# Two of eight pairs of output weight rows prepared inside the last expert, the others spread over sixteen chunks, and the last pair of token blocks finished product by product

## The chip, the core and the metric

The program runs on one core of one Trainium2 chip. The metric is the device time of one execution in microseconds (us). The engines are TensorE (PE in the rows; PEld is its weight load), VectorE (DVE), ScalarE (ACT), GpSimd (POOL) and SyncE (SP), which issues the loads.

## The reference, cut to what matters

Three layers run one after the other: a windowed attention, a mixture of eight experts of which each token takes one, and a dense layer with a squared rectifier. The change is in the third layer and in what is prepared for it.

```python
def _moe_ref(x, w_gate, w_output_gate, w1, w2):   # x: 2304 tokens x 512
    ...
    for e in range(E):                            # 8 experts
        mask = e_idx == e
        h = np.maximum(x[mask] @ w1[e], 0.0)      # 512 -> 1024
        ye = h @ w2[e]                            # 1024 -> 512
        out[mask] = gate_w[mask, None] * eom[mask, e, None] * ye

def _moe2_ref(x, w_in, w_out):
    h = x @ w_in                                  # 512 -> 2048
    r = np.maximum(h, 0.0)
    g = r * r
    return (g @ w_out).astype(np.float32)         # 2048 -> 512
```

The scale of a token (`gate_w` times `eom`) is positive, so the kernel leaves it out of the experts and multiplies its square onto the last layer's result (`gs`).

## The kernel before

Every float32 operand of a product is split into two float16 parts, hi and lo, and a product is three matmuls (hi by hi, hi by lo, lo by hi; `SPLIT`). ScalarE writes hi, VectorE then writes lo as operand minus hi.

**The experts.** Tokens are gathered expert by expert. Expert r has two layers on TensorE: eight groups for 1024 hidden rows (line 1172), then four groups for 512 outputs (line 1193), whose results go to `x2`. The experts take 264, 440, 248, 380, 284, 340, 304 and 320 tokens as columns. Beside the matmuls a `Stream` of small steps runs: pieces of the coming experts' weights are loaded by SP into four staging buffers and split (lines 300 and 301), and sixteen pieces of `w_in`, which arrive as 64-bit numbers, are decoded by three VectorE operations (lines 328, 332 and 336) and split (lines 342 and 343) into `wi`. `mixture` deals the `w_in` pieces to the 16 half-experts by a share called `spare`, in which the last expert counts twice; it gets 3 of the 16. The method `to(part, frac)` of the stream issues steps up to a fraction of a part, in program order, between the kernel's own instructions. An engine runs its instructions in that order.

**The dense layer.** The first four blocks of 128 tokens (`G0`) run plainly: for each of 16 chunks of 128 hidden rows, `plain1` makes h by 12 matmuls of 512 columns (line 1257), ScalarE squares it and VectorE splits it (line 1282), and `plain2` adds its product with `w_out` into four accumulators `acc`, 12 matmuls again (line 1289). `plain2` runs three chunks behind `plain1` (`AHEAD`), and takes the hidden rows n and n + 8 of pair n one after the other (`ORDER1`). The other 14 blocks run in seven pairs of blocks, each in 8 steps: `pair1` makes h for the hidden rows n and n + 8, and `pair2` multiplies 2 by 2 blocks with seven products in place of eight, into seven halves of the four banks `acc` (line 1327). For that, `shared_out` prepares `w_out` in eight pairs of hidden rows: two pieces decoded and split into `wo` (lines 342 and 343), four sums of 256 columns (line 376), and the sums split into `wt`. Its steps run in the plain stage, `bg.to(0, (i + 2) / NF)` ahead of the i-th `plain2`.

**The end of a pair of blocks.** After the last step n = 7 the seven products are combined: ScalarE copies p1 (line 1335), VectorE makes six sums (line 816), ScalarE scales two results by `gs` (line 1344), and GpSimd scatters them to the output (line 1248).

Of the kernel before, what the change touches and what calls it, by code (L numbers as in the profile page):

```python
# [114 lines left out]
def fused_kernel(ctx: ExitStack, tc: tile.TileContext, q, k, v, w_gate, w_ogate, w1, w2, w_in, w_out, out):  # L115
# [247 lines left out]
    def shared_out(wo, wt, tmp):  # L363

        res = []
        for n in range(HF):
            x = [None, None]

            def whole(i, n=n, x=x):
                parts(x[i](), wo[:, 0, n + HF * i, :], wo[:, 1, n + HF * i, :], WO_S)  # L370

            def sums(x=x):
# [5 lines left out]
            def sum_parts(n=n):  # L378
                parts(tmp, wt[:, 0, n], wt[:, 1, n], WO_S)

            if wide:
                src = w_out.bitcast(U32).rearrange("(k p) c -> k p c", p=P)
                for i in range(2):
                    st = {}
                    load, ops = decode64(src[n + HF * i], st)
                    x[i] = lambda st=st: st["d"].bitcast(F32)
                    res.append((load, ops + [lambda i=i, whole=whole: whole(i)] + [sums, sum_parts][:2 * i]))
            else:
                st = {}

                def load(n=n, st=st):
                    st["t"] = stage_p.tile([P, 1024], F32, tag="stage", name="stage")
                    for i in range(2):
                        k = n + HF * i
                        nc.sync.dma_start(out=st["t"][:, i * DM:(i + 1) * DM], in_=w_out[k * P:(k + 1) * P, :])
                for i in range(2):
                    x[i] = lambda i=i, st=st: st["t"][:, i * DM:(i + 1) * DM]
                res.append((load, [lambda whole=whole: whole(0), lambda whole=whole: whole(1), sums, sum_parts]))
        return res

# [403 lines left out]
    x2 = [w_p.tile([P, KC, XW], F16, name=f"x2{i}") for i in range(2)]  # L804

# [153 lines left out]
    wu = [g_p.tile([P, 8192], F16, name=f"wu{i}") for i in range(3)]  # L959
    xg = [g_p.tile([P, DM], F32, name=f"xg{i}") for i in range(4)]  # L960
# [156 lines left out]
    def mixture(caps, e_regs, first):  # L1117
# [167 lines left out]
    def plain2(n, g, ps):  # L1285
        f = ORDER1[n]
        for j in range(G0):
            for k, (a, o) in enumerate(SPLIT):
                nc.tensor.matmul(out=ps[j], lhsT=g[:, a, j * P:(j + 1) * P], rhs=wo[:, o, f, :],  # L1289
                                 start=n == 0 and k == 0, stop=n == NF - 1 and k == 2)  # L1290
# [28 lines left out]
    def pair2(u, n, g, ps):  # L1319
        for left, right, b, h in PRODUCTS:  # L1320
            for k, (a, o) in enumerate(SPLIT):
                if isinstance(right, tuple):
                    i, c = right
                    r = wo[:, o, n + HF * i, c * HD:(c + 1) * HD]
                else:
                    r = wt[:, o, n, right]
                nc.tensor.matmul(out=ps[b][:, h * HD:(h + 1) * HD], lhsT=g[:, a, left * P:(left + 1) * P], rhs=r,  # L1327
                                 start=n == 0 and h == 0 and k == 0,
                                 stop=n == HF - 1 and k == 2 and (h == 1 or b == 3))
        if n < HF - 1:  # L1330
            return
        (p1, p2), (p6, p7), (p5, p3), (p4, _) = [(x[:, 0:HD], x[:, HD:]) for x in ps]
        c1, u2, u3, v = [tmp[:, i] for i in range(4)]
        x1, x2_ = out_tile(), out_tile()
# [58 lines left out]
```

## Time and profile before

| what | us |
|---|---|
| median of 3 runs | 783.53 |
| the three runs | 783.53, 783.87, 779.66 |
| the profiled execution | 779.48 |
| its span, first to last instruction | 777.80 |
| in it: last expert, first and second layer | 349.09 to 376.5 |
| in it: the plain stage, 16 chunks | 376.55 to 498.41 |
| in it: seven pairs of blocks | 498.41 to 766.88 |
| in it: the last results' way out | 766.88 to 777.80 |
| TensorE busy over the span | 724.6 (93%) |
| VectorE busy over the span | 479.0 (62%) |
| ScalarE busy over the span | 398.8 (51%) |

The span leaves 1.68 us of the execution's own time outside. The granted TensorE clock is given as a share of full speed; its two levels are 1.2 and 2.4 GHz, and its mean over the span was 0.962. A busy TensorE is not TensorE at its peak: a matmul that waits inside, or runs at the lower clock, counts as busy.

### The profile page before, as it was taken

Reading aid. Unit: us, or ns where it says so; the run is one execution under the profiler, and the core shown is the slowest. Engines: PE = TensorE matmul, PEld = TensorE weight load, DVE = VectorE, ACT = ScalarE, POOL = GpSimd, SP = SyncE. Lnnn points to the kernel's source line nnn. Section 1 sums busy time; section 2 is a strip of 40 time slices with the busy share of each in tenths; the row PEclk is TensorE's granted clock in tenths of the full one; section 3 lists DMA queues with packets and bytes.
Section 4 is the critical chain, followed back from the end, with each engine's and each line's share of the span. In section 5 each row is a group of like instructions: output and inputs, shape, how many; then the busy total and the mean of one; then the engine's idle time right before and its main releaser. Section 6 shows DMA issues by size and latency. Waiting matters only on the chain.

```text
span 777.8 us, 16191 instructions
## 1 busy us (share of the span) xinstructions
PE 724.6 (93%) x6460; PEld 550.5 (71%) x6460; DVE 479.0 (62%) x1081; ACT 398.8 (51%) x762; POOL 68.9 (9%) x125
## 2 busy tenths in 40 slices
PE   7998997699999989999888887999999999999994
PEld 5877886385596677777433334788888888888883
DVE  4677678488689798765366667544444444454542
ACT  5786776265475465453434444544444444445351
POOL 8000002320110020000000000100000000000000
PEclk7999998599999999999989999899999999999998
DMA  9996543777676675652222220000000000000000
GB/s 218 203 220 152 128 105 86 236 241 264 198 252 212 200 238 183 212 162 73 85 81 82 81 82 0 29 28 14 15 14 15 8 22 1 29 1 29 1 28 28
DMA packets 74979, 82.74 MB, mean 106 GB/s; under 512 B 33784, under 2 KB 57848, under 8 KB 74896
## 3 DMA queue, kind: packets, MB, share of 16 engines
q1 hardware_dynamic: 71552, 71.61, 31.5%
q0 software_dynamic: 3344, 10.01, 3.7%
q8 instruction: 53, 0.87, 0.5%
q14 instruction: 30, 0.25, 0.1%
HBM read 72.16 MB, written 9.44 MB: 105 GB/s over the span
## 4 chain that ended last, share of the span: by engine, by line
PE 69%; DVE 11%; DMA 8%; ACT 8%; issue 3%; SPq 0%; POOL 0%; POOLq 0%; DVEq 0%; ACTq 0%
PE l L1257 18%; PE acc L1327 14%; PE bank L1193 13%; PE bank L1172 11%; DMA vt<-in_v_dram 3%; PE sps L584 2%; PE xps L629 2%; DMA q<-in_q_dram 2%; PE acc L1289 2%; PE tps L610 2%; ACT w L1266 1%; ACT w L1265 1%; DVE dec L336 1%; DVE dec L332 1%; PE bank L978 1%
## 5 line engine op out<-in xcount | busy, mean ns | idle before, releaser
L1257 PE MATMUL l<-x,wi 128*128 128x256 f16 (+1 forms) x1536 | 200.0, 286 | 1.2 <-DVE x L1199 1.2
L1257 PEld LDWEIGHTS <-wi 128*128 128x128 f16 x1536 | 150.5, 98 | 41.0 <-issue 3.1
L1327 PEld LDWEIGHTS <-gg 128*128 128x128 f16 x1176 | 114.9, 98 | 17.3 <-issue 3.1
L1193 PE MATMUL bank<-hs,wu 128*128 128x264 f16 (+7 forms) x768 | 109.3, 300 | 2.4 <-DVE hs L1176 2.2
L1172 PE MATMUL bank<-xs,wu 128*128 128x264 f16 (+7 forms) x768 | 108.6, 303 | 1.2 <-ACT wu L300 0.8
L816 DVE TENSOR_TENSOR w<-w 128x128 f32<-128x128 f32 x224 | 55.3, 288 | 81.4 <-ACT w L1266 79.0
L1172 PEld LDWEIGHTS <-wu 128*128 128x128 f16 x768 | 75.7, 99 | 32.3 <-ACT wu L300 1.1
L1311 DVE TENSOR_TENSOR gg<-w,gg 128x896 f16<-128x896 f32 x56 | 61.2, 1092 | 60.5 <-ACT gg L1310 60.5
L1193 PEld LDWEIGHTS <-wu 128*128 128x128 f16 x768 | 74.8, 98 | 31.9 <-issue 2.5
L1327 PE MATMUL acc<-wt,gg 128*128 128x256 f16 x672 | 92.6, 272 | 1.1 <-DVE A L816 0.5
L1310 ACT ACTIVATE gg<-w 128x896 f16<-128x896 f32 x56 | 53.2, 950 | 64.6 <-DVE w L816 64.6
L301 DVE SCALAR_TENSOR_TENSOR wu<-stage,wu 128x1024 f16<-128x1024 f32 (+1 forms) x68 | 75.8, 1127 | 12.5 <-ACT wu L300 11.9
L1265 ACT ACTIVATE w<-l 128x512 f32<-128x512 f32 x72 | 42.5, 591 | 64.5 <-PE l L1257 59.8
L1327 PE MATMUL acc<-wo,gg 128*128 128x256 f16 x504 | 73.3, 272 | 0.0
L1289 PE MATMUL acc<-wo,gg 128*128 128x512 f16 x192 | 52.0, 420 | 18.6 <-ACT wo L342 16.1
L300 ACT ACTIVATE wu<-stage 128x1024 f16<-128x1024 f32 (+1 forms) x68 | 65.3, 974 | 4.2 <-DMA stage<-in_moe_w_dram 4.2
L1289 PEld LDWEIGHTS <-gg 128*128 128x128 f16 x192 | 20.1, 105 | 47.7 <-issue 30.6
L1175 ACT ACTIVATE hs<-bank 128x264 f16<-128x264 f32 (+7 forms) x64 | 27.8, 436 | 39.6 <-PE bank L1172 39.6
L1266 ACT ACTIVATE w<-w 128x512 f32<-128x512 f32 x72 | 45.4, 630 | 2.3
L601 ACT ACTIVATE pr<-sps,mx 128x96 f32<-128x96 f32 x144 | 37.1, 349 | 13.0 <-DVE mx L592 9.6
L970 POOL DMA_INDIRECT xg<-x_dram,slot_i x24 | 27.0, 1127 | 152.8 <-PE bank L978 99.0
L1198 ACT ACTIVATE x<-bank 128x264 f32 (+7 forms) x32 | 14.1, 440 | 51.4 <-PE bank L1193 51.4
(192 smaller groups left out, 796.9 us busy)
## 6 DMA issues: line engine op xcount, KB each, us to landing
stage<-in_moe_w_dram SPq DMA_DIRECT2D x62, 512.0 KB
dstage<-in_moe_w_in_dram SPq DMA_DIRECT2D x16, 512.0 KB
dstage<-in_moe_w_out_dram SPq DMA_DIRECT2D x16, 512.0 KB
vt<-in_v_dram SPq DMA_DIRECT2D x56, 96.0 KB
q<-in_q_dram SPq DMA_DIRECT2D x16, 288.0 KB
k<-in_k_dram SPq DMA_DIRECT2D x16, 288.0 KB
x_dram<-xn SPq DMA_DIRECT2D x22, 128.0 KB
hs<-in_moe_w_dram SPq DMA_DIRECT2D x2, 512.0 KB
```

Source lines behind the costliest of these rows:

```text
L300: nc.scalar.activation(out=half(hi, n), in_=sv, func=AF.Copy, scale=scale)
L301: nc.vector.scalar_tensor_tensor(out=half(lo, n), in0=sv, scalar=scale, in1=half(hi, n), op0=ALU.mult, op1=ALU.subtract)
L816: V.tensor_tensor(out=out, in0=a, in1=b, op=op)
L1172: nc.tensor.matmul(out=ps, lhsT=w[:, a, k, f * P:(f + 1) * P], rhs=x[:, k, 0:C], start=nn == 0, stop=nn == 3 * KC - 1)
L1193: nc.tensor.matmul(out=ps, lhsT=w[:, a, f, c * P:(c + 1) * P], rhs=hs[:, o, f, 0:C], start=nn == 0, stop=nn == 3 * (F // P) - 1)
L1257: nc.tensor.matmul(out=ps, lhsT=wi[:, a, kc, f * P:(f + 1) * P], rhs=x2[o][:, kc, toks], start=nn == 0, stop=nn == 11)
L1265: nc.scalar.activation(out=flat[:, 512:], in_=ps, func=AF.Relu, scale=R_D)
L1266: nc.scalar.activation(out=flat[:, 0:512], in_=flat[:, 512:], func=AF.Square)
L1289: nc.tensor.matmul(out=ps[j], lhsT=g[:, a, j * P:(j + 1) * P], rhs=wo[:, o, f, :], start=n == 0 and k == 0, stop=n == NF - 1 and k == 2)
L1310: nc.scalar.activation(out=g[:, 0], in_=w7, func=AF.Copy)
L1311: V.tensor_tensor(out=g[:, 1], in0=w7, in1=g[:, 0], op=ALU.subtract)
L1327: nc.tensor.matmul(out=ps[b][:, h * HD:(h + 1) * HD], lhsT=g[:, a, left * P:(left + 1) * P], rhs=r, start=n == 0 and h == 0 and k == 0, st ...
```

## The change

The buffer `wu1`, one of three that hold expert weights, moves to a pool that lives on into the dense layer. `shared_out` takes a list of pairs and issues its steps one by one: hi of both pieces, the sums, hi of the sums, and then the lo parts. In the last expert, where no `w_in` piece remains, two pairs are prepared into `wu1`, one in each layer; the sixteen `w_in` pieces go to experts 0 to 6. The other six pairs are prepared in the plain stage into a tile `wp`, an equal share of steps ahead of each of the 16 chunks, beginning with the first. Of the last pair of blocks, the steps n = 6 and 7 are merged: each of the seven products runs over both before the next. At the end of every pair of blocks the scaling by `gs` goes into VectorE's sums, with three small ScalarE operations of 256 columns in place of two of 512, and the sums stand in another order; the fourth sum of `w_out` changes its sign, so that p4 is added.

```diff
-    def shared_out(wo, wt, tmp):
+    def shared_out(ns, wo, wt, tmp):
         res = []
-        for n in range(HF):
+        for n in ns:
...
-            def whole(i, n=n, x=x):
-                parts(x[i](), wo[:, 0, n + HF * i, :], wo[:, 1, n + HF * i, :], WO_S)
+            def hi(i, n=n, x=x):
+                nc.scalar.activation(out=wo(n)[:, 0, i], in_=x[i](), func=AF.Copy, scale=WO_S)
+
+            def lo(i, n=n, x=x):
+                nc.vector.scalar_tensor_tensor(out=wo(n)[:, 1, i], in0=x[i](), scalar=WO_S, in1=wo(n)[:, 0, i],
+                                               op0=ALU.mult, op1=ALU.subtract)
...
-                for out, p, q in ((t[0], b12, b11), (t[1], b22, t[0]), (t[2], b22, b12), (t[3], t[1], b21)):
-                    nc.vector.tensor_tensor(out=out, in0=p, in1=q, op=ALU.subtract)
+                out, p, q = ((t[0], b12, b11), (t[1], b22, t[0]), (t[2], b22, b12), (t[3], b21, t[1]))[m]
+                nc.vector.tensor_tensor(out=out, in0=p, in1=q, op=ALU.subtract)
...
+            ops = ([lambda m=m, sums=sums: sums(m) for m in range(4)]
+                   + [sum_hi, lambda lo=lo: lo(0), lambda lo=lo: lo(1), sum_lo])
...
-                    res.append((load, ops + [lambda i=i, whole=whole: whole(i)] + [sums, sum_parts][:2 * i]))
+                    res.append((load, dec + [lambda i=i, hi=hi: hi(i)] + ops * i))
...
-        spare = [max(caps[h // 2] - 240, 0) * (1 if h < 2 * E - 2 else 2) for h in range(2 * E)]
+        spare = [max(caps[h // 2] - 240, 0) * (h < 2 * E - 2) for h in range(2 * E)]
+        outs = shared_out(range(NE), lambda n: wo_part(wu1, n), lambda n: wt_part(wu1, n),
+                          xg_t[:, 0:2].rearrange("p a (s d) -> p (a s) d", s=2))
...
+            if h >= 2 * E - 2:
+                m = len(outs) // (2 * E - h)
+                part += outs[:m]
+                del outs[:m]
...
-    wo = m2_p.tile([P, 2, NF, DM], F16, name="wo")
-    wt = m2_p.tile([P, 2, HF, 4, HD], F16, name="wt")
-    tmp = m2_p.tile([P, 4, HD], F32, name="tmp")
-    bg = Stream([shared_out(wo, wt, tmp)])
+    wp = m2_p.tile([P, (HF - NE) * WP], F16, name="wp")
+    tmp = m2_p.tile([P, 5, HD], F32, name="tmp")
...
+    bg = Stream([shared_out(range(NE, HF), wo, wt, tmp[:, 0:4])])
...
-    def pair2(u, n, g, ps):
+    def pair2(u, ng, ps):
         for left, right, b, h in PRODUCTS:
-            for k, (a, o) in enumerate(SPLIT):
...
+            for n, g in ng:
+                for k, (a, o) in enumerate(SPLIT):
...
         nc.scalar.activation(out=c1, in_=p1, func=AF.Copy)
-        tt(x1[:, 0:HD], p2, c1, ALU.add)
+        nc.scalar.activation(out=c1g, in_=p1, func=AF.Copy, scale=g1)
         tt(u2, p6, c1, ALU.add)
         tt(u3, p7, u2, ALU.add)
+        nc.scalar.activation(out=u3, in_=u3, func=AF.Copy, scale=g0)
+        scaled(x1[:, 0:HD], p2, g1, c1g)
         tt(v, p5, u2, ALU.add)
-        tt(x2_[:, HD:], p5, u3, ALU.add)
-        tt(x1[:, HD:], p3, v, ALU.add)
-        tt(x2_[:, 0:HD], u3, p4, ALU.subtract)
-        for x, j in ((x1, u + 1), (x2_, u)):
-            nc.scalar.activation(out=x, in_=x, func=AF.Copy, scale=gs[:, j:j + 1])
-            send(x, j)
+        nc.scalar.activation(out=v, in_=v, func=AF.Copy, scale=g1)
+        scaled(x0[:, HD:], p5, g0, u3)
+        scaled(x1[:, HD:], p3, g1, v)
+        send(x1, u + 1)
+        scaled(x0[:, 0:HD], p4, g0, u3)
+        send(x0, u)
...
-        bg.to(0, (i + 2) / NF)
+        bg.to(0, (i + 1) / NF)
...
+        elif i < len(steps) - 2:
+            pair2(u, [(n, g_of.pop(i))], ps)
+        elif n == HF - 1:
+            pair2(u, [(m, g_of.pop(i + m - n)) for m in (n - 1, n)], ps)
```

**VectorE in the plain stage.** `gg` is the lo part of a chunk's squares, `dec` a decoded piece, `wo` and `wt` (before) or `wp` (after) the prepared rows. Before, two chunks and the pair between them:

```order
L1282 TENSOR_TENSOR gg<-w_8207,gg 128x512
L328 TENSOR_SCALAR dec<-dstage 128x512
L332 SCALAR_TENSOR_TENSOR dec<-dstage,dec 128x512
L336 SCALAR_TENSOR_TENSOR dec<-dstage,dec 128x512
L343 SCALAR_TENSOR_TENSOR wo<-dec,wo 128x512
L328 TENSOR_SCALAR dec<-dstage 128x512
L1282 TENSOR_TENSOR gg<-w_8248,gg 128x512
L332 SCALAR_TENSOR_TENSOR dec<-dstage,dec 128x512
L336 SCALAR_TENSOR_TENSOR dec<-dstage,dec 128x512
L343 SCALAR_TENSOR_TENSOR wo<-dec,wo 128x512
```

VectorE in the plain stage after the change, from the second to the third chunk:

```order
L1316 TENSOR_TENSOR gg<-w_8208,gg 128x512
L336 SCALAR_TENSOR_TENSOR dec<-dstage,dec 128x512
L381 TENSOR_TENSOR tmp<-dec 128x256
L381 TENSOR_TENSOR tmp<-dec,tmp 128x256
L381 TENSOR_TENSOR tmp<-dec 128x256
L381 TENSOR_TENSOR tmp<-dec,tmp 128x256
L1316 TENSOR_TENSOR gg<-w_8233,gg 128x512
L374 SCALAR_TENSOR_TENSOR wp<-dec,wp 128x512 x2
L387 SCALAR_TENSOR_TENSOR wp<-tmp,wp 128x1024
L328 TENSOR_SCALAR dec<-dstage 128x512
```

A lo part no longer stands right behind the decode whose hi part it waits for, and the preparation begins three chunks earlier.

**VectorE from expert 3 to expert 4.** `x_2755` is an expert's result, `wu` expert weights, `hs` the hidden rows that the second layer reads. Before:

```order
L1199 SCALAR_TENSOR_TENSOR x_2755<-bank,x_2754 128x380
L343 SCALAR_TENSOR_TENSOR wi<-dec,wi 128x512
L301 SCALAR_TENSOR_TENSOR wu_2886<-stage,wu_2886 128x1024
L1199 ISA
L1199 SCALAR_TENSOR_TENSOR x_2755<-bank,x_2754 128x380
L301 SCALAR_TENSOR_TENSOR wu_2886<-stage,wu_2886 128x1024 x2
L1176 SCALAR_TENSOR_TENSOR hs<-bank,hs 128x284
```

VectorE at the same place, after:

```order
L1227 SCALAR_TENSOR_TENSOR x_2755<-bank,x_2754 128x380
L301 SCALAR_TENSOR_TENSOR wu_2887<-stage,wu_2887 128x1024
L328 TENSOR_SCALAR dec<-dstage 128x512
L332 SCALAR_TENSOR_TENSOR dec<-dstage,dec 128x512
L1227 ISA
L1227 SCALAR_TENSOR_TENSOR x_2755<-bank,x_2754 128x380
L336 SCALAR_TENSOR_TENSOR dec<-dstage,dec 128x512
L343 SCALAR_TENSOR_TENSOR wi<-dec,wi 128x512
L301 SCALAR_TENSOR_TENSOR wu_2887<-stage,wu_2887 128x1024
L1204 SCALAR_TENSOR_TENSOR hs<-bank,hs 128x284
```

A second `w_in` piece has come into expert 3, and the end of it stands ahead of expert 4's first hidden rows.

**VectorE at the end of the last pair of blocks.** `A` and `ob` are the two result tiles. Before:

```order
L816 TENSOR_TENSOR A<-acc_11680,tmp 128x256
L816 TENSOR_TENSOR tmp<-acc_11681,tmp 128x256
L816 TENSOR_TENSOR tmp<-acc_11681,tmp 128x256
L816 TENSOR_TENSOR tmp<-acc_11682,tmp 128x256
L816 TENSOR_TENSOR ob_8070<-acc_11682,tmp 128x256
L816 TENSOR_TENSOR A<-acc_11682,tmp 128x256
L816 TENSOR_TENSOR ob_8070<-tmp,acc_11683 128x256
```

VectorE at the same place, after:

```order
L831 TENSOR_TENSOR tmp<-acc_11727,tmp 128x256
L831 TENSOR_TENSOR tmp<-acc_11727,tmp 128x256
L1374 SCALAR_TENSOR_TENSOR A<-acc_11726,gs,tmp 128x256
L831 TENSOR_TENSOR tmp<-acc_11728,tmp 128x256
L1374 SCALAR_TENSOR_TENSOR ob_8154<-acc_11728,gs,tmp 128x256
L1374 SCALAR_TENSOR_TENSOR A<-acc_11728,gs,tmp 128x256
L1374 SCALAR_TENSOR_TENSOR ob_8154<-acc_11729,gs,tmp 128x256
```

The operation that reads the first bank (the first row before) now stands third, and no operation of 512 columns follows on ScalarE.

## Rows read from the trace of the kernel before

**Rows 1.** The page, part 4: the chain that ended last, by engine

```profile
PE 69%; DVE 11%; DMA 8%; ACT 8%; issue 3%; SPq 0%; POOL 0%; POOLq 0%; DVEq 0%; ACTq 0%
```

**Rows 2.** Busy time by stretch; columns in the first row

```profile
core 0: us, PE busy (x) PEld busy (x) DVE busy (x) ACT busy (x) POOL busy (x), PEclk, DMA share, GB/s
...
277.90:293.14 15.24, 13.08 (x111) 10.56 (x110) 14.53 (x26) 9.69 (x17) 4.45 (x3) 1.00 0.80 263
...
362.13:376.55 14.42, 13.20 (x98) 9.33 (x96) 7.78 (x14) 3.96 (x8) 0.00 (x0) 1.00 0.08 18
376.55:498.41 121.86, 103.31 (x481) 48.70 (x482) 75.97 (x135) 54.02 (x83) 0.00 (x0) 0.93 0.19 64
498.41:757.70 259.29, 258.22 (x2343) 228.91 (x2342) 123.05 (x303) 122.98 (x177) 15.95 (x16) 1.00 0.05 17
```

**Rows 3.** Timeline of TensorE, plain stage: start, us, instruction, idle time before and its releaser

```profile
392.25 5.58 PE L1289 MATMUL acc<-wo,gg 128*128 128x512 f16 x12 [5.18 <-ACT wo L342]
...
405.97 0.38 PE L1289 MATMUL acc<-wo,gg 128*128 128x512 f16 x1
...
431.74 0.38 PE L1289 MATMUL acc<-wo,gg 128*128 128x512 f16 x1 [1.76 <-ACT wo L342]
```

**Rows 4.** The chain that ended last, plain stage and end: start, us, what

```profile
400.78 2.59 PE acc L1289 x12
403.37 2.60 PE l L1257 x12
...
768.67 0.27 issue
```

**Rows 5.** Groups by line, 376.55 to 498.41: busy us, mean ns, then idle before

```profile
L1289 PE MATMUL acc<-wo,gg 128*128 128x512 f16 x192 | 52.0, 420 | 18.6 <-ACT wo L342 16.1 <-DVE wo L343 2.1
...
L1282 DVE TENSOR_TENSOR gg<-w,gg 128x512 f16<-128x512 f32 x16 | 11.1, 692 | 21.4 <-ACT gg L1281 21.4
L336 DVE SCALAR_TENSOR_TENSOR dec<-dstage,dec 128x512 uint32<-128x512 uint32 x16 | 11.1, 692 | 0.6
L343 DVE SCALAR_TENSOR_TENSOR wo<-dec,wo 128x512 f16<-128x512 f32 x16 | 11.1, 692 | 11.1 <-ACT wo L342 11.1
...
L343 DVE SCALAR_TENSOR_TENSOR wt<-tmp,wt 128x1024 f16<-128x1024 f32 x8 | 9.8, 1226 | 9.0 <-ACT wt L342 9.0
...
L328 DVE TENSOR_SCALAR dec<-dstage 128x512 uint32<-128x512 uint32 x16 | 6.7, 420 | 0.0
L376 DVE TENSOR_TENSOR tmp<-dec 128x256 f32<-128x256 f32 x16 | 6.7, 419 | 0.0
```

**Rows 6.** Timeline of VectorE from expert 3 to expert 4

```profile
268.01 2.36 DVE L301 SCALAR_TENSOR_TENSOR wu<-stage,wu 128x1024 f16<-128x1024 f32 x2 [0.39 <-ACT wu L300]
270.29 0.45 DVE L1176 SCALAR_TENSOR_TENSOR hs<-bank,hs 128x284 f16<-128x284 f32 x1
```

**Rows 7.** Timeline of VectorE, end of the last expert

```profile
375.90 0.49 DVE L1199 SCALAR_TENSOR_TENSOR x<-bank,x 128x320 f32 x1
```

**Rows 8.** Timeline of VectorE and TensorE between two pairs of blocks

```profile
577.26 0.42 DVE L816 TENSOR_TENSOR ob<-acc,tmp 128x256 f32<-128x256 f32 x1
...
577.73 0.81 PE L1327 MATMUL acc<-wo,gg 128*128 128x256 f16 x6
...
579.51 0.49 PE L1327 MATMUL acc<-wt,gg 128*128 128x256 f16 x3 [0.18 <-DVE ob L816]
```

**Rows 9.** Timeline of all engines at the end of the program

```profile
766.39 0.49 PE L1327 MATMUL acc<-wt,gg 128*128 128x256 f16 x3
...
767.49 0.41 DVE L816 TENSOR_TENSOR A<-acc,tmp 128x256 f32<-128x256 f32 x1
...
768.93 0.97 POOL L1248 DMA_INDIRECT out_dram<-A,perm_i  x1 [24.27 <-ACT A L1344]
...
772.42 0.97 POOL L1248 DMA_INDIRECT out_dram<-ob,perm_i  x1 [2.52 <-DMA out_dram<-A,perm_i]
```

**Rows 10.** Timeline of ScalarE, plain stage

```profile
410.00 0.63 ACT L342 ACTIVATE wo<-dec 128x512 f16<-128x512 f32 x1 [2.08 <-DVE dec L336]
```

More of the change, by code (lines that the diff above doesn't have):

```diff
@@ L397, in shared_out @@
                     x[i] = lambda i=i, st=st: st["t"][:, i * DM:(i + 1) * DM]
-                res.append((load, [lambda whole=whole: whole(0), lambda whole=whole: whole(1), sums, sum_parts]))
+                res.append((load, [lambda i=i, hi=hi: hi(i) for i in range(2)] + ops))
         return res
+    NE = 2
+    WP = 4096
     sctx = ExitStack()
@@ L804, in fused_kernel @@
     x2 = [w_p.tile([P, KC, XW], F16, name=f"x2{i}") for i in range(2)]
+    wu1 = w_p.tile([P, 8192], F16, name="wu1")
     mctx = ExitStack()
@@ L958, in fused_kernel, with wo_part, wt_part @@
     g_p = mctx.enter_context(tc.tile_pool(name="g", bufs=1))
-    wu = [g_p.tile([P, 8192], F16, name=f"wu{i}") for i in range(3)]
-    xg = [g_p.tile([P, DM], F32, name=f"xg{i}") for i in range(4)]
+    wu = [wu1 if i == 1 else g_p.tile([P, 8192], F16, name=f"wu{i}") for i in range(3)]
+    xg_t = g_p.tile([P, 4, DM], F32, name="xg")
+    xg = [xg_t[:, i] for i in range(4)]
+    def wo_part(t, n):
+        return t[:, n * WP:n * WP + WP // 2].rearrange("p (o i d) -> p o i d", o=2, i=2)
+    def wt_part(t, n):
+        return t[:, n * WP + WP // 2:(n + 1) * WP].rearrange("p (o s d) -> p o s d", o=2, s=4)
     xs = [g_p.tile([P, 2, KC, max(CAP)], F16, name=f"xs{i}") for i in range(2)]
@@ L1229, in fused_kernel, with wo, wt @@
     HD = DM // 2
[L1230 to L1233 removed]
+    wp = m2_p.tile([P, (HF - NE) * WP], F16, name="wp")
+    tmp = m2_p.tile([P, 5, HD], F32, name="tmp")
+    def wo(n):
+        return wo_part(wu1, n) if n < NE else wo_part(wp, n - NE)
+    def wt(n):
+        return wt_part(wu1, n) if n < NE else wt_part(wp, n - NE)
+    bg = Stream([shared_out(range(NE, HF), wo, wt, tmp[:, 0:4])])
     Af = A.rearrange("p t m -> p (t m)").bitcast(F32)
@@ L1285, in plain2 @@
     def plain2(n, g, ps):
-        f = ORDER1[n]
+        i, f = divmod(ORDER1[n], HF)
         for j in range(G0):
             for k, (a, o) in enumerate(SPLIT):
-                nc.tensor.matmul(out=ps[j], lhsT=g[:, a, j * P:(j + 1) * P], rhs=wo[:, o, f, :],
+                nc.tensor.matmul(out=ps[j], lhsT=g[:, a, j * P:(j + 1) * P], rhs=wo(f)[:, o, i],
                                  start=n == 0 and k == 0, stop=n == NF - 1 and k == 2)
@@ L1317, in fused_kernel @@
                 (S4, (1, 1), 2, 1), (A22, 3, 3, 0))
-    def pair2(u, n, g, ps):
+    def pair2(u, ng, ps):
         for left, right, b, h in PRODUCTS:
-            for k, (a, o) in enumerate(SPLIT):
[L1322 to L1330, printed above, removed]
+            for n, g in ng:
+                for k, (a, o) in enumerate(SPLIT):
+                    if isinstance(right, tuple):
+                        i, c = right
+                        r = wo(n)[:, o, i, c * HD:(c + 1) * HD]
+                    else:
+                        r = wt(n)[:, o, right]
+                    nc.tensor.matmul(out=ps[b][:, h * HD:(h + 1) * HD], lhsT=g[:, a, left * P:(left + 1) * P], rhs=r,
+                                     start=n == 0 and h == 0 and k == 0,
+                                     stop=n == HF - 1 and k == 2 and (h == 1 or b == 3))
+        if ng[-1][0] < HF - 1:
@@ L1331, in pair2, with scaled @@
             return
         (p1, p2), (p6, p7), (p5, p3), (p4, _) = [(x[:, 0:HD], x[:, HD:]) for x in ps]
-        c1, u2, u3, v = [tmp[:, i] for i in range(4)]
-        x1, x2_ = out_tile(), out_tile()
+        c1, c1g, u2, u3, v = [tmp[:, i] for i in range(5)]
+        g1, g0 = gs[:, u + 1:u + 2], gs[:, u:u + 1]
+        x1, x0 = out_tile(), out_tile()
+        def scaled(out, x, g, y):
+            V.scalar_tensor_tensor(out=out, in0=x, scalar=g, in1=y, op0=ALU.mult, op1=ALU.add)
         nc.scalar.activation(out=c1, in_=p1, func=AF.Copy)
-        tt(x1[:, 0:HD], p2, c1, ALU.add)
+        nc.scalar.activation(out=c1g, in_=p1, func=AF.Copy, scale=g1)
@@ L1348, in fused_kernel @@
-    steps += [(pair1, (u, n), pair2, (u, n)) for u in range(G0, NB, 2) for n in range(HF)]
+        nc.scalar.activation(out=v, in_=v, func=AF.Copy, scale=g1)
[4 more added lines that the diff above has]
+        send(x0, u)
+    steps = [(None, n) for n in range(NF)] + [(u, n) for u in range(G0, NB, 2) for n in range(HF)]
     AHEAD = 3
@@ L1352, in fused_kernel @@
         if i < len(steps):
-            f, at = steps[i][:2]
-            g_of[i] = f(*at)
+            u, n = steps[i]
+            g_of[i] = plain1(n) if u is None else pair1(u, n)
+        bg.to(0, (i + 1) / NF)
         i -= AHEAD
@@ L1357, in fused_kernel @@
             continue
-        f, at = steps[i][2:]
-        bg.to(0, (i + 2) / NF)
-        if at[-1] == 0:
+        u, n = steps[i]
+        if n == 0:
             ps = acc()
-        f(*at, g_of.pop(i), ps)
+        if u is None:
+            plain2(n, g_of.pop(i), ps)
+        elif i < len(steps) - 2:
+            pair2(u, [(n, g_of.pop(i))], ps)
+        elif n == HF - 1:
+            pair2(u, [(m, g_of.pop(i + m - n)) for m in (n - 1, n)], ps)
 _INS = ["q", "k", "v", "moe_w_gate", "moe_w_output_gate", "moe_w1", "moe_w2", "moe2_w_in", "moe2_w_out"]
```

12 lines of the change are left out of this document (7 added, 5 removed).

## The prediction

> **What bounds the kernel now.** I read the page first, for what the end hangs on, then the busy time by stretch, then the timeline of the stretch in which TensorE idles, and last the order of the instructions there. The chain that ended last is TensorE's for 69% of the span [rows 1], so a gain must come from a stretch in which TensorE waits or runs slowly. The seven pairs of blocks aren't one: TensorE is busy for 258.22 of 259.29 us at full clock [rows 2]. The plain stage is: 103.31 busy of 121.86 us, at a mean clock of 0.93, while VectorE is busy for 75.97 and ScalarE for 54.02. No engine is full there, so the stage is bound by waits.
>
> Whose waits, the groups tell: `plain2` (line 1289) idles 18.6 us, 16.1 of it for ScalarE's hi parts of `wo` [rows 5]. The first product waits 5.18 us and then takes 5.58 us for 12 matmuls [rows 3], where the same 12 take 2.59 us elsewhere [rows 4]: after the wait they run at half the clock. Later it waits once a pair of rows: from 405.97 to 431.74 [rows 3] lie two pairs, 12.9 us each. VectorE explains that distance. One pair costs it two decodes of 0.42 + 0.69 + 0.69, two lo parts of 0.69, four sums of 0.42 and 1.23 for their lo part, 7.89 us, and 2 x 0.69 for the `gg` of the two chunks [rows 5], in all 9.27 us. To that come idle waits for hi parts, 11.1/16 twice and 9.0/8 once, 2.5 us. Together that is 11.8 us, and some hand-overs, against 2 x 5.19 = 10.4 us of TensorE [rows 4]. Since `plain2` needs each pair right when VectorE finishes it, TensorE follows VectorE's chain.
>
> **The change part by part.** The plain stage. TensorE's work stays: 16 chunks of 2.60 + 2.59 and three first halves of the pair stage, which hold as many columns, 3 x 2.60, are 90.8 us [rows 4]. VectorE's share falls to six pairs over 16 chunks, 6 x 7.89/16 + 0.69 = 3.65 us a chunk against 5.19. The lo parts stand behind other work, so the waits for hi are largely filled. The order gives six steps to each chunk, from the first one on; the fullest chunk holds its `gg`, three lo parts and two operations of a decode, 0.69 + 0.69 + 0.69 + 1.23 + 0.42 + 0.69 = 4.4 us. Pair n (2 to 7) is finished in chunk 3, 6, 8, 11, 14 and 16, and its first product stands behind chunk 8, 10, 12, 14, 16 and 18: two chunks or more to spare, 10 us. Pairs 0 and 1 exist before the stage. So no wait for `wo` should be left, and with the waits the half clock behind them goes. I take the floor: 90.8 - 121.86 = **-31.0**. The ceiling is that each of six pairs still costs what it does now beyond TensorE, 12.9 - 10.4 = 2.5 us, together 15.
>
> The last expert. Three `w_in` pieces leave, 3 x 2.49 us of VectorE, and two pairs come, 2 x 7.89. VectorE was busy for 7.78 of 14.42 us in the second layer [rows 2], so it fits there with one of the pairs and two pieces less. The second layer's last steps, two sums and three lo parts, stand between the third group's result and the fourth's. From the third result's lo part, a group of TensorE ahead of the last at some 373.1, I count two sums (0.8), the wait for their hi part (9.0/8 = 1.1, in which the two lo parts of 0.69 run) and the lo part of 1.23 [rows 5], which ends at about 376.2; the last result's lo part stands at 375.90 now [rows 7], and the dense layer waits for it. **+0.3**; between 0 and 3 x 0.69 + 1.23, if none of it is covered, 3.3. On SP's queue four loads of `w_out` stand here in place of three of `w_in`; with a DMA share of 0.08 [rows 2] they cost nothing.
>
> Experts 1, 3 and 5 get one `w_in` piece more each, 2.49 us of VectorE plus 0.63 of ScalarE [rows 5, 10]. In experts 1 and 5 I cover it by VectorE's idle time there and by the hidden rows' slack ahead of the second layer. Behind expert 3 there is no cover: VectorE is full from 268.01 [rows 6], and expert 4's second layer already loses 15.24 - 13.08 = 2.16 us [rows 2] to late `hs`. Now the end of the second piece, 0.69 + 0.69 and the wait of 0.65 for its hi part, takes the place of one weight part of 2.36/2 us [rows 6], and the first `hs` goes from 270.29 to about 271.3. What is queued behind it are all eight `hs`, and TensorE waits for the last two. **+1.0**; between 0 and 3 x 2.49 = 7.5.
>
> The end of each pair of blocks. The next pair's first product writes the first half of a bank and starts at 577.73, when VectorE's read of the other half of that bank ends, 577.26 + 0.42 [rows 8]. So the bank is what it waits for. The Trainium skill ("PSUM — Partial Sum Buffer", section "PSUM bank collisions raise a hardware error") has the rule that speaks against this change: guard by bank, not by address. By addresses the first product would need only ScalarE's copies, and the six crossings would cost nothing, 1.5 us less in the sum below; the row agrees with the page. In the new order that read stands third, after two sums of 0.42 that overlap a little: it ends some 0.72 us later, and the first product starts as much later. In return the wait inside the seven products goes, which is for the third bank: 12 matmuls at 258.22/2343 = 0.11 us [rows 2] would bring TensorE there at 579.05, and it comes at 579.51 [rows 8]. By the time the new order asks for the later banks they are free. Net 0.72 - 0.46, some 0.25 us, times six crossings: **+1.5**; between 0 and 6 x 0.72 = 4.3.
>
> The last end. The last matmul ends at 766.39 + 0.49 = 766.88, the first scatter starts at 768.93, the second 3.49 us behind it whatever its data did [rows 9]. So the end hangs on the first scatter. By products, the third bank is complete one product of six matmuls ahead of the end, 0.66 us, at 766.22; then come VectorE's sum v (0.42), ScalarE's scaling of 256 columns (0.4, as 512 take 0.63 [rows 10]), VectorE's last operation (0.41 [rows 9], though it multiplies too) and the hand-over to GpSimd (0.27 [rows 4]), with small gaps: 767.85. That is **-1.1**; between 0, if VectorE's queue is late, and -1.8, if each product could be read as it ends. The merged steps need the last `gg`, which is ready when they begin.
>
> Sum: -31.0 + 0.3 + 1.0 + 1.5 - 1.1 = -29.3, against the profiled 779.48 (1.68 us of it outside the span, which stay): 750.2. The three runs are 783.53, 783.87 and 779.66, so the profiled one is at the low end of a gap of 4 us. A half-clock stretch costs up to 3.0 us (5.58 for 2.59 [rows 3, 4]), and how many waits tip the clock may differ from run to run, which one trace can't show; then the gap goes with the stage. If it lies elsewhere it stays. I take most of it as gone: **751**.
>
> **The rivals.** One: VectorE is fuller in experts 1 to 6 than I count, and the three pieces are exposed whole: 7.5 in place of 1.0, **757.5**. For it speaks that VectorE is busy for 14.53 of 15.24 us in expert 4's second layer [rows 2]; against it, that this is the fullest stretch.
>
> Two: the plain stage is only half healed. VectorE and ScalarE wait for each other inside each chunk, and the six pairs keep their 2.5 us: 751 + 15 = **766**. Against it speaks the spare time of two chunks.
>
> Three, the slow side: `wp` is one tile for six pairs, and a product could wait for the last write into the tile that stands ahead of it in the program, which is the same chunk's. After the chunk's first half, that write takes ScalarE's three operations and the `gg`, 0.6 to 0.69 each [rows 5, 10], and some 3 us of VectorE's share: 5.5 us in place of none, 16 times 88 us, **839**. It decides from 29.3/16 = 1.8 us a chunk on. Against it: `wo` is one tile today, and the third chunk's product started at 405.97 [rows 3] although a write to `wo` that stands ahead of it came only at 410.00 [rows 10]. So waits go by the piece.
>
> **How the numbers follow.** The forecast, 746.5 to 757 by itself, has 0.84; rival one 0.08, two 0.05, three 0.02, and 0.01 is left for no change. The low end has the last end at its best and the losses in the experts and at the crossings at nothing, 779.48 - 31.0 - 1.8 = 746.7, and 746.5 is given. The high end, 758, takes in rival one. About 0.5% is what a measurement of this kernel can tell from no change: faster 0.97, within 0.5% 0.01, slower 0.02.
>
> **What would show it.** Right: in the plain stage of the new profile TensorE is busy throughout, at a clock of 1.00, and the stage takes 91 us; line 1289's successor has no idle time for `wo` or `wp`. Expert 4's second layer idles some 3 us, up from 2.16. At a crossing the first product starts 0.7 us later after the VectorE read than now, and the seven products run without a gap. The first scatter of the last pair starts 1 us after the last matmul, not 2.05. Wrong: idle time in front of `plain2`, a clock under 0.97 in that stage, or gaps of several us in experts 2 to 6.

## The result and the profile after the change

The changed kernel takes 759.75 us (median of four, 758.3 to 760.37) against 781.88 (779.66 to 783.87): a ratio of 0.9715, with a 95% interval of 0.9679 to 0.9751. The sign and the place of the gain were forecast; the time lies 1.75 us above the range's end of 758. The profiled execution took 760.0 us, 758.2 of it the span.

The chain of the changed kernel that ended last, by engine as in [rows 1], then its busy time by stretch: last expert, plain stage, pairs of blocks and the way out (columns as in [rows 2]):

```profile
PE 79%; DVE 7%; DMA 6%; issue 4%; ACT 3%; SPq 0%; POOLq 0%; POOL 0%; DVEq 0%; ACTq 0%
```

```profile
350.85:381.07 30.22, 26.24 (x195) 18.72 (x193) 22.32 (x42) 11.42 (x21) 0.00 (x0) 0.97 0.36 121
381.07:476.88 95.81, 95.81 (x481) 47.56 (x482) 59.99 (x109) 49.65 (x79) 0.80 (x1) 0.97 0.13 45
476.88:748.16 271.28, 266.23 (x2426) 237.00 (x2423) 128.50 (x312) 126.56 (x189) 15.10 (x16) 1.00 0.05 17
748.16:758.20 10.04, 0.00 (x1) 0.00 (x0) 1.08 (x3) 0.35 (x1) 1.94 (x2) 0.66 0.14 53
```

TensorE is now busy through the whole plain stage, where [rows 2] had 103.31 of 121.86 us, and its share of the chain rises from the 69% of [rows 1] to 79%. Stage by stage, the two profiled executions against the forecast:

| stage | before, us | after, us | forecast | measured |
|---|---|---|---|---|
| up to the first expert | 149.25 | 149.93 | 0 | +0.68 |
| experts 0 to 3 | 117.04 | 117.39 | 0 | +0.35 |
| expert 4 | 26.85 | 27.57 | +1.0 | +0.72 |
| experts 5 and 6 | 55.95 | 55.96 | 0 | 0.0 |
| last expert, up to the dense layer | 27.46 | 30.22 | +0.3 | +2.76 |
| plain stage | 121.86 | 95.81 | -31.0 | -26.05 |
| seven pairs of blocks | 268.47 | 271.28 | +1.5 | +2.81 |
| last results' way out | 10.92 | 10.04 | -1.1 | -0.88 |
| sum | 777.80 | 758.20 | -29.3 | -19.6 |

Of the difference of 9.7 us, 7.4 lie at the plain stage and at its door; 1.3 lie in the pairs. The groups of TensorE by shape within the plain stage of the changed kernel (columns as in [rows 5]):

```profile
L1291 PE MATMUL l<-x,wi 128*128 128x512 f16 x192 | 46.0, 394 | 4.0 <-issue 4.0
L1323 PE MATMUL acc<-wp,gg 128*128 128x512 f16 x144 | 33.0, 379 | 0.0
L1291 PE MATMUL l<-x,wi 128*128 128x256 f16 x96 | 11.1, 273 | 0.0
```

No product waits for prepared rows any more (0.0, where [rows 5] had 18.6). The last row is a count that the prediction had wrong: 96 matmuls of 256 columns are four first halves of the pair stage, of 24 each, not three. The first row has 4.0 us of idle time ahead of the stage, for nothing that the profile names. The timeline of TensorE at that door, and VectorE's last result there:

```profile
363.89 13.20 PE L1221 MATMUL bank<-hs,wu 128*128 128x320 f16 x96
381.07 12.97 PE L1291 MATMUL l<-x,wi 128*128 128x512 f16 x48 [3.98 <-issue]
```

```profile
377.82 0.48 DVE L1227 SCALAR_TENSOR_TENSOR x<-bank,x 128x320 f32 x1
```

The last result is there at 378.30, 1.21 us behind TensorE's last matmul (377.09); before, it came 1.06 us behind (376.39 and 375.33), and the dense layer began 0.16 us later. So VectorE's work in the last expert costs 0.15 us. But TensorE begins only at 381.07, 2.77 us behind the result. And the first 48 matmuls then take 12.81 us to the next group's start, where 4 x 2.59 = 10.36 were due: 2.4 us more, at a granted clock of 0.81 in that stretch:

```profile
381.07:393.88 12.81, 12.81 (x49) 5.28 (x50) 4.03 (x7) 4.23 (x7) 0.00 (x0) 0.81 0.14 44
```

What runs while TensorE stands still are loads. SP issues the first three for the plain stage at 373.02, 4.07 us ahead of the last matmul's end; before the change it issued them at 374.49, 0.84 us ahead of it. The DMA queues of the changed kernel from 375 to 378, then from 378 to 381.07, and of the kernel before from 373 to 375.4 (packets, MB, share of 16 engines):

```profile
q1 hardware_dynamic: 284, 1.03, 89.5%
```

```profile
q1 hardware_dynamic: 70, 0.23, 19.3%
q14 instruction: 3, 0.02, 2.6%
q8 instruction: 1, 0.02, 2.3%
```

```profile
q8 instruction: 1, 0.02, 3.1%
```

Instructions come by DMA too. Before, a packet of them passed ahead of the loads; now none passes while the loads hold the engines for 89.5% of the time, and four come behind. The Trainium skill ("Runtime: NRT & Kernel Launch", section "Instruction fetch mechanics") says that a taken branch whose target hasn't been fetched waits for a DMA of its instructions. Here the experts stand in one of two branches, and every engine leaves it to reach the dense layer. The trace agrees as far as it goes: the one packet on q8 starts at 378.47, 1.38 us behind the last matmul, and TensorE begins 2.60 us behind that start. That is theory A: the loads come before the fetch and delay it. Theory B: the gap comes from the jump itself, or from what VectorE still has to do.

### The profile page after: what moved, and what is told of

Its sections match the earlier page's. It is cut to its first block, busy times and chain, and to the rows that moved or that the text cites. A ratio compares the mean times of both kernels' runs of the same rounds, so it can differ in the third digit from the quotient of the medians.

```text
span 758.2 us, 16198 instructions
## 1 busy us (share of the span) xinstructions
PE 717.5 (95%) x6460; PEld 550.2 (73%) x6460; DVE 478.8 (63%) x1081; ACT 398.5 (53%) x769; POOL 68.7 (9%) x125
## 4 chain that ended last, share of the span: by engine, by line
PE 79%; DVE 7%; DMA 6%; issue 4%; ACT 3%; SPq 0%; POOLq 0%; POOL 0%; DVEq 0%; ACTq 0%
PE l L1291 23%; PE acc L1363 15%; PE bank L1221 12%; PE bank L1200 12%; PE acc L1323 5%; PE sps L598 3%; PE tps L570 2%; DMA k<-in_k_dram 2%; PE xps L643 2%; PE tps L624 2%; DVE wu L301 1%; PE bank L1000 1%; DMA xg<-x_dram,slot_i 1%; DVE w L831 1%; ACT gg L1344 1%
## 5 line engine op out<-in xcount | busy, mean ns | idle before, releaser
L1363 PEld LDWEIGHTS <-gg 128*128 128x128 f16 x1176 | 115.0, 98 | 19.9 <-issue 6.1
L1363 PE MATMUL acc<-wp,gg 128*128 128x256 f16 x882 | 102.7, 273 | 0.0
L301 DVE SCALAR_TENSOR_TENSOR wu<-stage,wu 128x1024 f16<-128x1024 f32 (+1 forms) x68 | 75.7, 1126 | 10.3 <-ACT wu L300 9.4
L1363 PE MATMUL acc<-wu,gg 128*128 128x256 f16 x294 | 34.9, 272 | 5.1 <-DVE A L1374 2.5
L1204 DVE SCALAR_TENSOR_TENSOR hs<-bank,hs 128x264 f16<-128x264 f32 (+7 forms) x64 | 30.9, 487 | 8.5 <-ACT hs L1203 8.3
L1282 POOL DMA_INDIRECT out_dram<-A,perm_i x9 | 9.0, 1000 | 298.5 <-ACT A L1328 161.7
```

Of the source, the lines that this page charges most:

```text
L301: nc.vector.scalar_tensor_tensor(out=half(lo, n), in0=sv, scalar=scale, in1=half(hi, n), op0=ALU.mult, op1=ALU.subtract)
```

## The experiments

| kernel | median, us | ratio to before, 95% interval |
|---|---|---|
| after_again | 759.56 | 0.9731 (0.9669 to 0.9794) |
| late_loads | 757.12 | 0.9700 (0.9644 to 0.9757) |
| old_end_inside | 757.04 | 0.9688 (0.9631 to 0.9745) |
| all_in_plain | 770.24 | 0.9865 (0.9807 to 0.9923) |
| early_loads | 754.56 | 0.9677 (0.9650 to 0.9704) |
| deal_as_before | 758.59 | 0.9750 (0.9705 to 0.9795) |
| last_steps_apart | 760.84 | 0.9783 (0.9748 to 0.9818) |
| three_repairs | 751.57 | 0.9647 (0.9621 to 0.9674) |
| four_repairs | 750.50 | 0.9615 (0.9591 to 0.9639) |
| old_end_merged | 759.67, one run | no interval |

The times of one kernel spread over 2 to 8 us, so what follows is read from stages of the traces. A part of that spread lies ahead of everything that was changed: line 964, which no kernel here alters, starts at 136.07 in one trace and at 140.21 in another.

### The changed kernel again

> The changed kernel once more, unaltered. Theory A (TensorE's first instructions of the dense layer arrive late, because three loads of w_out, issued 1.5 us sooner than before, hold the DMA queues just then): the gap of 4.0 us ahead of the dense layer and the half clock behind it (48 matmuls in 12.8 us instead of 10.4) are in every execution, and the times stay at 758 to 761 us. If the gap was chance, an execution without it takes 755 us.

The gap is there again, 4.10 us, with 12.05 us for the 48 matmuls; in all six traces of kernels that leave this place alone (the two of the changed kernel and four below) it is 3.7 to 4.7 us. It isn't chance.

### The first loads later

```diff
-                    load, dec = decode64(src[n + HF * i], st)
+                    load, dec = decode64(src[n + HF * i], st, nc.scalar if len(res) < late else nc.sync)
...
-    bg = Stream([shared_out(range(NE, HF), wo, wt, tmp[:, 0:4])])
+    bg = Stream([shared_out(range(NE, HF), wo, wt, tmp[:, 0:4], 4)])
```

The number 4 is `late`: the first four loads for the plain stage go from SP's queue to ScalarE's, and no others.

> The changed kernel, except that the first four loads of w_out for the plain stage are issued by ScalarE behind the squares of the first chunk, so that nothing is loaded while the experts end. Theory A: the gap ahead of the dense layer falls from 4.0 to 1.2 to 1.5 us, the clock stays full behind it, and 2.6 + 2.4 us go: 755 us. Theory B (the gap comes from what VectorE still does behind the last expert, two pairs of rows, or from the longer way to the code itself): the gap stays 4.0 us and the time 760 us. If only the clock's part is something else: 757 us.

Timeline of TensorE at the door of the dense layer and in the plain stage, and of VectorE there:

```profile
381.39 10.52 PE L1291 MATMUL l<-x,wi 128*128 128x512 f16 x48 [1.36 <-DVE x L1227]
...
466.50 2.54 PE L1323 MATMUL acc<-wp,gg 128*128 128x512 f16 x11 [1.79 <-DVE wp L374]
```

```profile
465.76 1.28 DVE L374 SCALAR_TENSOR_TENSOR wp<-dec,wp 128x512 f16<-128x512 f32 x2
```

The gap falls to 1.36 us and ends with VectorE's result, and the 48 matmuls run at full clock. VectorE's work in the last expert and the branch are as they were: theory A holds, B falls. The edit changes the queue of the loads with their time; the next experiment leaves the queue alone. The 5 us did not all arrive: with the loads later, the last pair is late by 1.79 us, and the plain stage takes 95.91 us.

### The first loads sooner

```diff
-                m = len(outs) // (2 * E - h)
+                m = 3 if h == 2 * E - 2 else 1
```

> The changed kernel, except that of the four loads for the two pairs prepared in the last expert, three belong to its first layer and one to its second, so that the last decode ends some 2.5 us sooner, and with it the first loads for the plain stage come sooner. Theory A: the loads are through (371 to 376 us after the start, if the stages ahead take what they took in the changed kernel's first profile) when TensorE's next instructions are fetched; the gap ahead of the dense layer is 1.4 to 2 us instead of 4.0 to 4.7, the clock stays full, and unlike with the late loads no product in the plain stage waits for its rows: 36 x 2.59 = 93.4 us for the stage. Rival: the jump out of the branch itself, or VectorE's two pairs, make the gap: 4 us as before.

```profile
375.26 1.28 SPq L321 DMA_DIRECT2D dstage<-in_moe_w_out_dram  x3
```

```profile
383.10 10.52 PE L1291 MATMUL l<-x,wi 128*128 128x512 f16 x48 [1.70 <-DVE x L1227]
```

```profile
383.10:476.45 93.35, 93.35 (x480) 46.93 (x481) 59.99 (x109) 49.64 (x79) 0.79 (x1) 1.00 0.14 46
```

The last matmul of the experts ends at 381.40 here; the loads are issued 6.1 us ahead of that, and their last packets start at 381.27. The gap is 1.70 us, the clock is full, and the plain stage is 93.35 us, 16 x 5.19 + 4 x 2.60. Loads issued 0.84 or 6.1 us ahead of the last matmul's end, or 5.6 us behind it, leave no gap of 4 us, and loads 4 us ahead do.

What the loads delay shows in the packets of q8. Of this queue one packet of instructions passes at the door in every trace; here it is in the changed kernel (378.25 to 378.75), in late_loads (378.5 to 379.0) and in early_loads (380.5 to 381.0):

```profile
q8 instruction: 1, 0.02, 13.8%
```

```profile
q8 instruction: 1, 0.02, 15.8%
```

```profile
q8 instruction: 1, 0.02, 12.1%
```

In the six traces with the gap it starts 1.2 to 2.1 us behind the experts' last matmul. Where nothing is being loaded then (before, late_loads, all_in_plain) it starts 1.5 us ahead of that, and in early_loads and the two kernels with all repairs, below, 0.6 to 0.8 us ahead, as their loads end. In all twelve traces TensorE's first matmul of the dense layer comes 2.5 to 2.8 us behind this packet's start. The profile does not name the engine of a queue, but its counts do. In the changed kernel q8 brings 19 packets in the seven pairs, where TensorE has 4849 instructions with its weight loads (the row for 476.88 to 748.16 above): 255 a packet. In the plain stage packets come at 389.1, 416.6 and 444.3, with some 255 of TensorE's instructions between two of them again. VectorE and ScalarE together have 26 a packet in the pairs and some 60 in the plain stage. So these packets are TensorE's code, and the gap follows from one of them coming late.

The packet also shows what is left. The profile puts the 1.70 us down to VectorE's result, but that is there at 382.45, and TensorE begins 0.65 us behind it, where it was 0.16 in the kernel before. Loads issued 6.1 us ahead still hold the packet back, for some 0.5 us.

### All eight pairs in the plain stage

```diff
-        outs = shared_out(range(NE), lambda n: wo_part(wu1, n), lambda n: wt_part(wu1, n),
-                          xg_t[:, 0:2].rearrange("p a (s d) -> p (a s) d", s=2))
+        outs = []
...
-    bg = Stream([shared_out(range(NE, HF), wo, wt, tmp[:, 0:4])])
+    bg = Stream([shared_out(range(HF), wo, wt, tmp[:, 0:4])])
```

> The changed kernel, except that no pair is prepared in the last expert; all eight are prepared in the plain stage, eight steps to a chunk, in the same buffers. Theory A, with VectorE not the bound (8 x 7.89 / 16 + 0.69 = 4.6 us a chunk against TensorE's 5.19): the loads land long before the experts end, so there is no gap and no half clock, and no wait for the rows: 755 us, and the two pairs in the last expert are worth nothing. Rival: VectorE is too full with eight pairs, and each pair keeps the 2 to 2.5 us that it cost before the change: 770 to 775 us.

No gap (1.20 us), as theory A has it, but the plain stage takes 108.22 us. Timeline of ScalarE, VectorE and TensorE over one pair:

```profile
417.59 1.06 ACT L384 ACTIVATE wp<-tmp 128x1024 f16<-128x1024 f32 x1 [2.22 <-DVE tmp L381]
418.21 2.53 PE L1322 MATMUL acc<-wp,gg 128*128 128x512 f16 x11 [1.35 <-DVE wp L374]
...
427.26 0.69 DVE L1315 TENSOR_TENSOR gg<-w,gg 128x512 f16<-128x512 f32 x1 [2.50 <-ACT gg L1314]
```

ScalarE's hi part of the sums waits 2.22 us for VectorE's four sums, with the squares of the next chunk queued behind it; VectorE waits 2.50 us for a chunk's squares, with the four sums of the next pair queued behind that. The two engines go round in 11.9 us a pair (from 418.21 to the same wait at 430.07), where TensorE needs 10.4 and VectorE's own operations 9.3. So the spreading and the new order of the steps together bring 121.86 to 108.22, and the two pairs taken out bring the rest, 108.22 to 93.4 without the door's loss: taking them out is needed, though VectorE has idle time with all eight.

### The old end at the first six crossings

```diff
+        if u < NB - 2:
+            x1, x2_ = out_tile(), out_tile()
+            nc.scalar.activation(out=c1, in_=p1, func=AF.Copy)
+            tt(x1[:, 0:HD], p2, c1, ALU.add)
...
+            return
```

What is left out are the sums and scalings of the kernel before, with p4 added.

> The changed kernel, except that the first six pairs of blocks end as before the change (six sums in the old order, two scalings of 512 columns by ScalarE); only the last pair ends in the new order. If the new order costs at the crossings what the two traces say (40.38 us a pair against 39.92), six times 0.46 = 2.8 us go: 757 us. Rival: the crossing is set by something that the order leaves alone (the gg of the next pair, the clock): no change, 760 us.

The seven pairs take 268.52 us, 2.76 less than after, and the wait inside the products is back. Row of TensorE at a crossing:

```profile
562.56 1.14 PE L1363 MATMUL acc<-wu,gg 128*128 128x256 f16 x9 [0.18 <-DVE ob L831]
```

In the changed kernel, VectorE's reading of the first bank and the first product behind it were

```profile
557.04 0.47 DVE L1374 SCALAR_TENSOR_TENSOR ob<-acc,gs,tmp 128x256 f32<-128x256 f32 x1
...
557.43 0.41 DVE L831 TENSOR_TENSOR tmp<-acc,tmp 128x256 f32<-128x256 f32 x1
557.57 2.53 PE L1363 MATMUL acc<-wu,gg 128*128 128x256 f16 x21 [0.84 <-DVE ob L1374]
```

Against [rows 8]: the read ended 3.56 us behind the start of the next first half (553.95), before 2.73 (577.68 behind 574.95), so +0.83; the seven products ran for 2.37 us up to the next first half in place of 2.76, so -0.39. Net 0.44, and 40.38 us from crossing to crossing against 39.92.

### The end of the program

The first kernel runs the last two steps one after the other; the second keeps them merged and ends every pair in the order of the kernel before:

```diff
-        elif i < len(steps) - 2:
+        else:
             pair2(u, [(n, g_of.pop(i))], ps)
-        elif n == HF - 1:
-            pair2(u, [(m, g_of.pop(i + m - n)) for m in (n - 1, n)], ps)
```

> The changed kernel, except that the steps n = 6 and 7 of the last pair of blocks run one after the other, as in the other pairs; the new order at the pair's end stays. If the merging is worth what the prediction says, one more product of three matmuls ahead of the end: from the last matmul to the end 0.33 us more, 10.0 to 10.3 us, out of 10.9 before the change. Rival: the whole gain at the end is the order's: 10.0 us. The median can't tell these apart, the trace can.

```diff
-        if u < NB - 2:
+        if True:
```

The second diff is against old_end_inside.

> The changed kernel, except that all pairs of blocks, the last too, end in the order and with the scalings of the kernel before; the last two steps stay merged. From the last matmul to the end: 9.97 us with both parts of the change, 10.93 with the new order alone. If the merging is worth the whole gain, 10.0 us; if the new order is needed beside it (VectorE's half of 256 columns and no scaling of 512 columns behind it), 10.3 to 10.9 us. The crossings take 39.92 us a pair, as in the kernel before.

Last matmuls and first scatter of the changed kernel, of the new order alone, and of the merging alone:

```profile
744.83 3.33 PE L1363 MATMUL acc<-wp,gg 128*128 128x256 f16 x29
...
749.31 0.97 POOL L1282 DMA_INDIRECT out_dram<-A,perm_i  x1 [24.12 <-DVE A L1374]
```

```profile
740.76 4.31 PE L1363 MATMUL acc<-wp,gg 128*128 128x256 f16 x38
...
747.14 0.97 POOL L1282 DMA_INDIRECT out_dram<-A,perm_i  x1 [25.05 <-DVE A L1374]
```

```profile
742.82 4.42 PE L1363 MATMUL acc<-wp,gg 128*128 128x256 f16 x39
...
748.74 0.97 POOL L1282 DMA_INDIRECT out_dram<-A,perm_i  x1 [23.72 <-ACT A L1381]
```

From the last matmul's end to the first scatter: 1.15 us with both, 2.07 with the order alone, 1.50 with the merging alone, and 2.05 before [rows 9]. The order alone is worth nothing: VectorE's sums then begin only 0.87 us ahead of the last matmul's end, where with both it is 1.85. The merging is worth 0.55, and only then the order another 0.35. The first expectation was off: without the merging 0.92 us are lost, not 0.33. The second named the outcome, 10.34 us in its 10.3 to 10.9. It rests on one run, and like every split here on one trace of each kernel.

The first of the two kernels also has the gap without the slow clock, from TensorE's timeline:

```profile
380.44 10.52 PE L1291 MATMUL l<-x,wi 128*128 128x512 f16 x48 [3.80 <-issue]
```

### Expert 4

```diff
-            n = round(len(shared_in(wi)) * sum(spare[:h + 1]) / sum(spare)) - n_s
-            n_s += n
+            n = (0, 1, 3, 3, 0, 0, 2, 1, 1, 0, 2, 1, 1, 1, 0, 0)[h]
```

> The changed kernel, except that the w_in piece that the change put into expert 3's second layer goes to expert 1's first layer. If that piece is what delays expert 4's hidden rows, expert 4 takes 26.85 us again (27.57 to 29.06 with the piece), and expert 1 stays at 36.53: 0.7 to 2.2 us. Rival: expert 4 is longer because of the clock or of a neighbour's load, and stays at 27.6 to 29.1.

TensorE's waits in expert 4's second layer, in the changed kernel and here:

```profile
283.31 0.52 PE L1221 MATMUL bank<-hs,wu 128*128 128x284 f16 x3 [1.49 <-DVE hs L1204]
285.22 0.40 PE L1221 MATMUL bank<-hs,wu 128*128 128x284 f16 x2 [1.39 <-DVE hs L1204]
```

```profile
281.78 0.52 PE L1220 MATMUL bank<-hs,wu 128*128 128x284 f16 x3 [0.77 <-DVE hs L1203]
283.69 0.40 PE L1220 MATMUL bank<-hs,wu 128*128 128x284 f16 x2 [1.39 <-DVE hs L1203]
```

The piece costs 0.72 us; expert 4 takes 26.84 us without it, as before, and expert 1 with one more stays at 36.53. So much is the waits. But in six of the eight traces that have the piece in expert 3, expert 4 took 28.9 to 30.5 us, with waits like these. The row of early_loads behind them:

```profile
287.92 5.36 PE L1221 MATMUL bank<-hs,wu 128*128 128x284 f16 x24
```

24 matmuls in 5.36 us, where 3.06 is usual: a granted clock of 0.55 behind two short waits, in some executions and not in others.

### The repairs together

> The changed kernel with three repairs together: the loads for the plain stage sooner (as in early_loads), the w_in piece in expert 1 (as in deal_as_before), and the old order of sums at the first six crossings (as in old_end_inside). If the three causes are separate, their gains add: 2.6 us of gap, some 2 us of half clock, 0.7 to 2.2 us in expert 4, 2.75 us at the crossings, 8 to 9.5 us in all: 750 to 752 us, at the end of a stage ahead of the experts that varies by 3 us. If they share a cause, less: 754 to 756 us.

751.57 us, as expected if the gains add. Gap 1.96 (TensorE begins 0.90 us behind VectorE's result, so the packet is still late), plain stage 93.36, pairs 268.52; expert 4 took 28.52 in this trace, with its old waits and some slow clock behind them.

```diff
-            n = (0, 1, 3, 3, 0, 0, 2, 1, 1, 0, 2, 1, 1, 1, 0, 0)[h]
+            n = (0, 1, 3, 3, 0, 0, 2, 1, 0, 0, 2, 2, 1, 1, 0, 0)[h]
```

> As three_repairs, and the w_in piece of expert 4's first layer goes to expert 5's second layer, so that VectorE has 2.5 us less ahead of expert 4's last hidden rows. If those rows are late only by VectorE's load, the two idle times there (0.77 + 1.39 = 2.16 us) fall to nothing or 0.3 us, the half clock that followed them by chance (0 to 2.9 us in the traces so far) goes with them, and expert 4 takes 24.7 to 25 us instead of 26.85 to 30.45; expert 5 stays at 29.03: 748 to 750 us. Rival: the piece is then late in expert 5, whose second layer pays what expert 4's saved: 751.5 us as before.

```profile
283.09 0.40 PE L1220 MATMUL bank<-hs,wu 128*128 128x284 f16 x2 [1.31 <-DVE hs L1203]
```

One of the two waits is gone and the other stays, so half of what was expected: expert 4 takes 25.84 us at a clock of 1.00, expert 5 stays at 29.03, and the median is 750.50. TensorE still begins the dense layer 0.76 us behind VectorE's result. That is the fastest kernel here, at a ratio of 0.9615 where the changed kernel had 0.9715 and 0.9731. All of the change is kept but the places of two `w_in` pieces and of one `w_out` load with its decode, and the order of sums at six of seven ends of pairs.

## Why the prediction was wrong

**The plain stage's floor: miscounted.** "Three first halves of the pair stage" are four. With three chunks of lead, the loop issues the first half of step i ahead of the second half of step i - 3, so that the fourth first half stands ahead of the first `pair2`. The floor was 16 x 5.19 + 4 x 2.60 = 93.4, not 90.8: 2.6 us, seen as 93.35 or 93.36 in the four kernels without half clock or waits there. It could have been read from the trace of before, by counting matmuls of 256 columns in that stretch.

**The loads: the step that failed.** "On SP's queue four loads of `w_out` stand here in place of three of `w_in`; with a DMA share of 0.08 [rows 2] they cost nothing." The four loads cost nothing, but the three behind them, for the plain stage, go out when the last decode in the expert frees their buffers, and that decode now ends earlier against the last matmul. They hold back the packet with TensorE's next instructions, a transfer that the prediction did not have at all. The price was 2.6 us of standing still and 2.4 us of half clock behind it. The share of 0.08 was an average over a stretch whose last microsecond mattered.

**The spare time: right in effect, wrong in size.** "Two chunks or more to spare, 10 us" was counted in chunks of the program. The last pair's lo parts and its first product in the changed kernel's trace:

```profile
464.23 1.28 DVE L374 SCALAR_TENSOR_TENSOR wp<-dec,wp 128x512 f16<-128x512 f32 x2
```

```profile
466.46 2.75 PE L1323 MATMUL acc<-wp,gg 128*128 128x512 f16 x12
```

The first of the two lo parts is done at some 464.9, 1.5 us ahead of the product, and loads that come later (late_loads) use that up. Rival two, that VectorE and ScalarE wait for each other inside each chunk, named the true mechanism; with eight pairs it decides (all_in_plain), with six it just doesn't.

**The crossings: right mechanism, sizes off.** 0.72 - 0.46 = 0.25 was 0.83 - 0.39 = 0.44 a crossing, since the third operation multiplies too (0.47 for 0.42) and the two sums hardly overlap: +2.8 us for +1.5.

**Expert 3 to 4: right in the waits, lucky in the time.** +0.72 for +1.0, with 2.88 us of idle time where some 3 was named, and nothing to speak of in experts 1 and 5; rival one falls. What was left out is that half clock can follow these waits, up to 3 us more. The profiled execution had none; six of the other seven with this order had it, and then the stage was 2 to 3.6 us longer than before. With the old waits, half clock is in one trace of three (three_repairs), too few to say what the change does to it.

**The last end: right.** -0.88 for -1.1, by the merging first and the order second.

**The slow side** fell as argued: no product waits for another's rows, so waits go by the piece.

**The rest**, 1.0 us, lies ahead of expert 4: 0.68 ahead of the first expert, which the change doesn't touch, and 0.35 in experts 0 to 3, where expert 1's first matmul waits 0.29 us for ScalarE in this trace and not in the second one of the same kernel. The range took in the whole exposure of three pieces, but no loss from loads at the door of the dense layer.

## What to carry to other kernels

Where a branch ends, look at what the DMA queues hold in the microseconds before it, and at which buffer's release sends the next loads: work moved ahead of that place moves the loads too, and the next instructions come behind them. Count the groups of matmuls in a stretch from the trace before calling their sum a floor. Slack counted in the program's order is not slack in time when two engines feed each other, and an order that helps the program's end should be tried at the inner ends by itself.

## What the runs showed of the hardware

Loads that hold the DMA engines for 89.5% of the time kept TensorE 2.6 us from the first instruction behind a branch, with its operands ready; with the same loads 2 us sooner some 0.5 us of this were left, and with loads much later nothing. In twelve traces of twelve the first matmul behind the branch came 2.5 to 2.8 us behind the start of one packet of instructions (0.02 MB on q8), which itself started between 1.5 us ahead of the last matmul of the branch and 2.1 us behind it. After a standstill of 3.7 to 4.7 us, TensorE's next 48 matmuls took 11.84 to 13.06 us in five traces of six and 10.36 in the sixth; after 1.2 to 2.0 us they took 10.35 to 10.36 in five of five. Behind two waits in expert 4, of 0.8 or 1.5 us and of 1.4 us, the slower level came in some executions and not in others, and it made up most of the spread of that stage, 26.8 to 30.5 us.
